# Logarithms of three chunks made in the step that sums them, and their alpha loaded one step later

## The chip, the cores and the metric

The kernel runs on one core of one Trainium2 chip. The metric is the device time of a run in microseconds. An engine is named as the profile names it: PE is TensorE (PEld its weight loads), DVE is VectorE, ACT is ScalarE, POOL is GpSimd, SP is SyncE, which here only issues DMAs.

## What is computed

The first half is a gated linear attention recurrence for 4 batches, 8 heads, 768 positions and a head width of 48. The second half is a feed-forward block on the result, 3072 tokens wide 384, with an inner width of 1024. Cut to its core, the reference is:

```python
for t in range(S):
    state = alpha[:, :, t, :, None] * state + np.einsum('bhd,bhe->bhde', k[:, :, t], v[:, :, t])
    y[:, :, t] = np.einsum('bhd,bhde->bhe', q[:, :, t], state)
x = y.transpose(0, 2, 1, 3).reshape(B * S, H * D)
a = x @ w1
b = x @ w2
h = a * b @ w3
out = h @ w_out
```

The weights arrive in float64; the rest is float32.

## The kernel before

**Chunks.** The 768 positions of a batch are cut into 6 chunks of 128, so there are 24 chunks, numbered 0 to 23 (chunk 8 is the ninth). Within a chunk the recurrence becomes matrix products: the logarithm of alpha is taken, summed over the positions with a triangular matrix, and turned back into decays that scale k and q.

**One chunk's path.** `load_a`, `load_kq` and `load_v` load alpha, k with q, and v. `logs` takes the logarithm on ACT (L302). From chunk 10 on (`LATE`), it also splits it into two parts, a copy on ACT (L306) and a difference on DVE (L307), so that the sum runs in two faster products. `decays` sums on PE (L318, L321 or L324, by the kind of chunk) and takes two exponentials on ACT (L327, L328). `decayed` scales k and q on DVE (L337). `transposed` transposes them on PE (L359) and copies them back on ACT (L361). `scores` forms the products of k and q (L399) and masks them on DVE (L402). `attend_state` applies the state (L419), `attend` the masked scores (L425), and copies the result out on ACT (L429). `outer` makes the new state (L371, then L379 or L381). `advance` decays the state on POOL (L388 to L390), from a few rows that travel through DRAM as `ends` (stores L309, L330, L332) and come back by L345.

**Pairs.** Chunks 2 to 7 come two at a time: one load of alpha and one logarithm serve two chunks, so that only even numbers load. All others load singly (L142), into the tile `ac`, which has two buffers. A load into a buffer waits until the logarithm, and the store L309 where there is one, have read what was in it.

**Steps.** The loop `for n in range(N + 1)` is the order of the work: step n computes the scores of chunk n, attends chunk n-1, transposes chunk n+1, scales chunk n+2, sums chunk n+3, and issues loads for later ones. `FIRST` is 6. Beside this, steps 0 to 6 convert w1 and w2 from float64 (L221 to L243, loads `raw` by L213); `third` makes the third part of some of these weights by two products on PE (L254, L255) and a copy on ACT (L256).

**The feed-forward part.** The results of chunks go to DRAM by `store` (`xd`), three chunks form a group, and `load_x` brings a group back (`xT`). `split_x` splits it into three parts, one on ACT (L447), two on DVE (L448, L449). `gate` multiplies it with the weights on PE (L455). From step 6 on, gates are pieces that fill PE between the recurrence's products. After the last chunk come the remaining gates, the folding of w3 with w_out, and the last projection.

**What sets the order.** Each engine and each DMA queue runs its instructions in the order in which the built program holds them. A planner derives it from the order of the calls and from its own estimate of times; `after_marks` names instructions after which a piece may stand. So a moved call may move other calls' instructions too. All matrix results go through 8 PSUM banks (`bank`), reused in turn: a product that gets a bank waits until its last reader is done. SP issues its DMAs in order, each waiting for the one that used its completion lane eight DMAs before.

The edit touches two places of the loop: the load of alpha at the step's head, and the two calls of `logs`.

Of the kernel before, what the change touches and what calls it, by code (L numbers as in the profile page):

```python
# [48 lines left out]
def kernel(  # L49
# [59 lines left out]
    def after_marks(*names):  # L109
        stack = ExitStack()  # L110
        for x in names:
            stack.enter_context(tc.issue_after(mark[x]))
        return stack
# [12 lines left out]
    def rows(src, n):  # L126
        b, c = divmod(n, NCH)
        return src[b, :, ds(c * C, C), :].rearrange("h p d -> p h d")

    def paired(n):  # L130
        return 2 <= n < PAIRED

    def load_a(n):
        if paired(n):
            if n % 2 == 0:
                b, c = divmod(n, NCH)
                x = pairs[n // 2 % 2]
                nc.sync.dma_start(out=x.rearrange("p h s d -> p h (s d)"), in_=alpha[b, :, ds(c * C, 2 * C), :].rearrange("h (p s) d -> p h (s d)", s=2))
                st["a", n] = st["a", n + 1] = x
        elif n < N:  # L140
            st["a", n] = inp.tile([C, H, D], FP32, tag="ac", name="ac", bufs=2)
            nc.sync.dma_start(out=st["a", n], in_=rows(alpha, n))  # L142

    def load_kq(n):
        if n >= N:
            return
        st["kq", n] = inp.tile([C, 2, H, D], FP32, tag="kq", name="kq")
        nc.sync.dma_start(out=st["kq", n][:, 0], in_=rows(k, n))
        nc.sync.dma_start(out=st["kq", n][:, 1], in_=rows(q, n))

    def load_v(n):
        if n < N:
            st["v", n] = vs[n % len(vs)]
            (nc.gpsimd if 2 < n < 8 else nc.sync).dma_start(out=st["v", n][:, :, 0:D], in_=rows(v, n))
# [103 lines left out]
    def fetch(ahead=3):  # L258
        while weights and len(begun) < ahead:
            begun.append(weights.popleft())  # L260
            next(begun[-1])
# [17 lines left out]
    def store():  # L279

        while later:
            dst, src = later.popleft()
            nc.sync.dma_start(out=dst, in_=src)
# [4 lines left out]
    def logs(n):  # L288
        if n >= N:
            return  # L290
        a = st.pop(("a", n))
        if paired(n):
            if n % 2 == 0:
                nc.scalar.activation(a, a, AF.Ln)
                st["la", n] = st["la", n + 1] = a
                b, c = divmod(n, NCH)
                if n in ends:
                    nc.gpsimd.dma_start(out=ends[n][2:3].rearrange("m (h d) -> m h d", h=H), in_=alpha[b:b + 1, :, c * C, :])
            return
        a = a.rearrange("p h d -> p (h d)")  # L300
        la = st["la", n] = work.tile([C, DM], FP32, tag="la", name="la")
        nc.scalar.activation(la, a, AF.Ln)  # L302
        if n >= LATE:

            t = st["la", n] = work.tile([C, 2, DM], FP32R, tag="la2", name="la2", bufs=1)
            nc.scalar.copy(t[:, 0], la)  # L306
            nc.vector.tensor_sub(t[:, 1], la, t[:, 0].bitcast(FP32))  # L307
        if n in ends:
            nc.gpsimd.dma_start(out=ends[n][2:3], in_=a[0:1])  # L309
# [83 lines left out]
    def scores(n):  # L393
        qkT = st["qkT", n]
        sc = [bank().rearrange("p (j c) -> p j c", j=NP) for _ in range(2)]
        for j in range(NP):
            for i in range(2):
                r = ds(DP * i, D)
                nc.tensor.matmul(sc[i][:, j, :], qkT[r, 0, j, :], qkT[r, 1, j, :], start=True, stop=True)  # L399
        ms = work.tile([C, 2, NP, C], FP32, tag="ms", name="ms")  # L400
        for i in range(2):
            masked = nc.vector.tensor_tensor(ms[:, i].bitcast(I32), sc[i].bitcast(I32), keep_bc, op=ALU.bitwise_and)  # L402
        ends_of_part1[0] = mark["ms", n] = masked.ins
        st["ms", n] = ms
# [3 lines left out]
    def attend_state(n):  # L408
        qkT = st.pop(("qkT", n))

        y = [bank()[:, 0:HP * C].rearrange("p (j c) -> p j c", c=C) for _ in range(2)]
        st["y", n] = y, [(half * HP + j, i, y[i][ds(DP * half, DP), j, :])
                         for j in range(HP) for i in range(2) for half in range(2)]
        if n % NCH:
            for j, i, to in st["y", n][1]:
                r = ds(DP * i, D)
                nc.tensor.matmul(to, Ts[n % 2][r, j, :], qkT[r, 1, j, :],  # L419
                                 start=(j % HP == 0), stop=False, skip_group_check=True)  # L420
# [18 lines left out]
    def load_x(g, queue=nc.sync):  # L439
        st["xT", g] = xp.tile([C, KM, TG], FP32, tag="xT", name="xT")  # L440
        queue.dma_start(out=st["xT", g], in_=xd[g].rearrange("(k p) t -> p k t", p=C))
# [157 lines left out]
    def run(pieces):  # L599

        for _ in range(pieces):
            if not fill:
                return
            try:
                next(fill[0])
            except StopIteration:
                fill.popleft()
# [22 lines left out]
    FIRST = 6  # L630
# [3 lines left out]
    for n in range(N + 1):  # L634
        store()
        if n in loads:
            load_x(loads[n])
        if n != 1:
            load_a(n + 5)
        raws = (3, 3, 3, 3, 2, 2, 3, 3)[n] if n < 8 else 4  # L640
        for m in (n + 3,) * (n <= FIRST) + (n + 4,) * (n >= FIRST):
            load_kq(m)
            if n < FIRST - 2:
                fetch(raws)
        if n >= FIRST:
            load_v(n + 2)
        if n:
            attend_state(n - 1)
        if n < N:
            scores(n)  # L650
        transposed(n + 1)
        if n == 1:
            decays(3)
            load_a(6)
            with after_marks(("e", 3)):
                logs(4)
        if n == FIRST + 1:
            run(2)
        if n < FIRST:
            with after_marks("pool"):  # L660
                load_v(n + 2)
        if n - 2 in begin and n > FIRST:
            g, tiles = begin[n - 2]
            with after_marks(("ms", n), ("qkT", n + 1)):
                split_x(g, 0)
            fill.extend(gate(g, f) for f in tiles)
        if n == FIRST:
            with after_marks("l", ("qkT", n + 1)):
                split_x(0, 0)
            fill.extend(gate(0, f) for f in begin[n - 3][1])  # L670
        pieces = ((3, 3, 2, 0) if n > FIRST + 3 else (0, 3, 3, 0))[(n - FIRST) % 4] if n >= FIRST else 0
        if n == 0:
            with after_marks(("qkT", 0)):
                logs(2)
            decays(2)
            with after_marks(("e", 2)):
                logs(3)
        early, ready = n < FIRST, len(thirds) if n > 2 else n // 2
        marks = (*[("qkT", n + 1)] * (n < N - 1), *[("qk", n + 1), ("ms", n)] * early, *["x3"] * (n - 2 in begin and n > FIRST))
        if n < N - 2 and n != FIRST:  # L680
            with after_marks(*marks):
                convert(2 if early else 1, raws)
        advance(n)
        if n:
            attend(n - 1)
        outer(n)
        if n > FIRST:
            third(ready)
        run(pieces > 0)
        if early:  # L690
            with after_marks(*marks):
                convert(1, raws)
        with after_marks(*[("ms", n)] * (n < 3)):
            decayed(n + 2)
        if not early:
            with after_marks(*[("qkT", n + 1)] * (n < N - 4)):
                logs(n + 4)
        if n == 4:
            load_x(0)
        convert(early and n > 0, raws)  # L700
        run(pieces > 1)
        if n:
            decays(n + 3)
        if n <= FIRST:
            third(ready)
        if 0 < n < FIRST:
            with after_marks(("e", n + 3)):
                logs(n + 4)
        if n == FIRST:
            with after_marks("x3", ("e", n + 3)):  # L710
                convert(2, raws)
        elif n < N - 2:
            convert(n == FIRST - 1 if early else n % 3 == 0, raws)
        if n == FIRST - 1:
            assert len(done) == 2 * KM
        run(pieces > 2)
        if n == N - 3:
            while begun:
                convert(1)
            weights.extend(load_out(j) for j in range(KF))  # L720
            fetch(4)
# [91 lines left out]
```

## Time and profile before

| | us |
|---|---|
| median of 3 runs | 473.2 |
| lowest and highest | 473.17, 474.83 |
| the profiled execution's own time | 471.82 |
| its span | 470.1 |
| PE busy | 456.8 (97%) |
| DVE busy | 358.2 (76%) |
| ACT busy | 278.6 (59%) |
| POOL busy | 78.4 (17%) |

Of the chain that ended last, 92% is PE's and 3% DMA's; L455 alone is 72% of the span. The profile's page cuts the span in 40 equal slices of some 11.75 us and gives each engine's busy share in tenths, and PE's granted clock in tenths of full speed. A timeline lists instructions in order of time: start, duration, engine, line of the kernel, operation, what it writes and reads, shapes; in brackets, how long the engine had been idle before it and what released it. A line of waits gives an engine and line, what it waited for, the total time, the number of times and the longest. A line of stretches gives for each its length, the busy time of PE, PEld, DVE, ACT and POOL with the number of instructions, then PE's granted clock, the DMA engines' share and the GB/s moved.

### The profile page before, as it was taken

Reading aid. Unit: us, or ns where it says so; the run is one execution under the profiler, and the core shown is the slowest. Engines: PE = TensorE matmul, PEld = TensorE weight load, DVE = VectorE, ACT = ScalarE, POOL = GpSimd, SP = SyncE. Lnnn points to the kernel's source line nnn. Section 1 sums busy time; section 2 is a strip of 40 time slices with the busy share of each in tenths; the row PEclk is TensorE's granted clock in tenths of the full one; section 3 lists DMA queues with packets and bytes.
Section 4 is the critical chain, followed back from the end, with each engine's and each line's share of the span. In section 5 each row is a group of like instructions: output and inputs, shape, how many; then the busy total and the mean of one; then the engine's idle time right before and its main releaser. Section 6 shows DMA issues by size and latency. Waiting matters only on the chain.

```text
span 470.1 us, 10039 instructions
## 1 busy us (share of the span) xinstructions
PE 456.8 (97%) x3848; PEld 433.3 (92%) x3848; DVE 358.2 (76%) x578; ACT 278.6 (59%) x552; POOL 78.4 (17%) x149
## 2 busy tenths in 40 slices
PE   4998999999999999999999999999999999999996
PEld 2676799999989989999999999999999999999996
DVE  2797996999969797999999968764641977766671
ACT  4686956767677464889887656644553633333330
POOL 5144212024102310222221111111111000000000
PEclk9999999999999999999999999999999999999999
DMA  9999999999999943566686432212013885555511
GB/s 179 243 216 233 237 219 207 228 225 217 218 214 222 254 124 101 178 192 203 207 287 176 158 122 101 85 50 85 33 52 117 245 238 185 175 162 167 173 52 50
DMA packets 145663, 80.29 MB, mean 171 GB/s; under 512 B 96240, under 2 KB 137456, under 8 KB 145616
## 3 DMA queue, kind: packets, MB, share of 16 engines
q1 hardware_dynamic: 139840, 64.44, 55.3%
q0 software_dynamic: 5776, 15.22, 10.4%
q8 instruction: 30, 0.49, 0.5%
q14 instruction: 17, 0.14, 0.1%
HBM read 57.58 MB, written 22.06 MB: 169 GB/s over the span
## 4 chain that ended last, share of the span: by engine, by line
PE 92%; DMA 3%; ACT 3%; DVE 1%; issue 0%; SPq 0%; DVEq 0%; ACTq 0%
PE bank L455 72%; PE bank L399 5%; PE bank L425 4%; PE bank L359 2%; PE bank L419 2%; PE bank L371 2%; PE bank L318 2%; PE bank L557 1%; DMA xd<-x 1%; PE bank L324 1%; DMA xT<-xd 1%; PE bank L321 1%; DMA ac<-in_alpha_dram 1%; DVE qk L337 0%; ACT e L327 0%
## 5 line engine op out<-in xcount | busy, mean ns | idle before, releaser
L455 PE MATMUL bank<-x,w 128*128 128x384 f32 x1152 | 211.9, 338 | 0.4 <-ACT rest L221 0.4
L455 PEld LDWEIGHTS bank<-x,w 128*128 128x128 f32 x1152 | 200.1, 188 | 2.6 <-ACT rest L221 0.7
L455 PE MATMUL bank<-w3o,ab 128*128 128x384 f32 x576 | 100.2, 336 | 0.0
L455 PEld LDWEIGHTS bank<-w3o,ab 128*128 128x128 f32 x576 | 99.9, 188 | 0.0
L480 ACT ACTIVATE bank<-bank 128x384 f32<-128x384 f32 x96 | 45.8, 477 | 41.0 <-PE bank L455 40.7
L464 ACT ACTIVATE t<-bank 128x384 f32<-128x384 f32 x64 | 31.4, 493 | 55.9 <-PE bank L455 54.7
L530 POOL DMA_DIRECT2D abd<-ab x45 | 26.1, 579 | 145.1 <-DVE ab L516 126.4
L516 DVE TENSOR_TENSOR ab<-bank,r 128x384 f32<-128x384 f32 x44 | 24.3, 553 | 25.2 <-ACT bank L480 15.2
L361 ACT COPY qkT<-bank 128x512 f32<-128x512 f32 x48 | 26.0, 591 | 23.4 <-PE bank L359 23.4
L586 DVE TENSOR_TENSOR ab<-abl,ab 128x1024 fp32r<-128x1024 f32 x24 | 29.4, 1224 | 12.8 <-ACT ab L585 12.8
L585 ACT ACTIVATE ab<-abl 128x1024 fp32r<-128x1024 f32 x24 | 25.5, 1061 | 21.0 <-PE bank L455 17.9
L455 PE MATMUL bank<-wo,w3T 128*128 128x384 f32 x192 | 35.9, 334 | 0.0
L455 PEld LDWEIGHTS bank<-wo,w3T 128*128 128x128 f32 x192 | 33.5, 188 | 0.0
L337 DVE TENSOR_TENSOR qk<-kq,e 128x768 f32<-128x768 f32 x24 | 23.5, 980 | 12.0 <-ACT e L328 8.7
L402 DVE TENSOR_TENSOR ms<-bank,keep 128x512 int32<-128x512 int32 x48 | 31.0, 680 | 0.8 <-PE bank L399 0.6
L466 DVE SCALAR_TENSOR_TENSOR o<-bank,t 128x384 f32<-128x384 f32 x24 | 13.4, 556 | 22.4 <-issue 13.8
L226 ACT ACTIVATE power<-power,rebias 128x512 uint32<-128x512 uint32 (+1 forms) x36 | 25.1, 700 | 8.9 <-DVE power L225 8.8
L587 DVE SCALAR_TENSOR_TENSOR ab<-ab,abl 128x1024 fp32r<-128x1024 f32 x24 | 29.2, 1217 | 0.0
L466 DVE SCALAR_TENSOR_TENSOR r<-bank,t 128x384 f32<-128x384 f32 x40 | 22.0, 551 | 9.5 <-ACT t L464 8.9
L399 PEld LDWEIGHTS bank<-qkT 48*128 48x128 f32 x384 | 24.3, 194 | 5.3 <-issue 2.2
L399 PE MATMUL bank<-qkT 48*128 48x128 f32 x384 | 29.0, 292 | 0.0
L425 PE MATMUL bank<-ms,v 128*64 128x128 f32 x384 | 27.1, 285 | 0.0
(88 smaller groups left out, 583.8 us busy)
## 6 DMA issues: line engine op xcount, KB each, us to landing
raw<-in_moe_w_dram SPq DMA_DIRECT2D x28, 512.0 KB, 5.4
abl<-abd SPq DMA_DIRECT2D x24, 512.0 KB, 4.4
abd<-ab POOLq DMA_DIRECT2D x45, 192.0 KB, 3.1
xT<-xd POOLq DMA_DIRECT2D x9, 576.0 KB, 4.5
kq<-in_k_dram SPq DMA_DIRECT2D x24, 192.0 KB, 5.4
kq<-in_q_dram SPq DMA_DIRECT2D x24, 192.0 KB, 5.4
xd<-x SPq DMA_DIRECT2D x48, 96.0 KB, 4.2
out_dram<-o SPq DMA_DIRECT2D x24, 192.0 KB, 3.5
```

Of the source, the lines that this page charges most:

```text
L361: mark["qkT", n] = nc.scalar.copy(qkT[:, :, :, ds(DP * half, DP)], tp[half]).ins
L399: nc.tensor.matmul(sc[i][:, j, :], qkT[r, 0, j, :], qkT[r, 1, j, :], start=True, stop=True)
L402: masked = nc.vector.tensor_tensor(ms[:, i].bitcast(I32), sc[i].bitcast(I32), keep_bc, op=ALU.bitwise_and)
L425: nc.tensor.matmul(to, vc[:, 2 * j + i, :], ms[:, i, j, :], start=(n % NCH == 0 and j % HP == 0), stop=(j % HP == HP - 1), skip_group_chec ...
L455: nc.tensor.matmul(p, w[part][i], x[part][i], start=start and part == parts[0] and i == 0, stop=stop and part == parts[-1] and i == n - 1, ...
L464: nc.scalar.activation(t, p1, AF.Copy, scale=(1.0 + 1.0 / P) * scale)
L466: nc.vector.scalar_tensor_tensor(to, p2, scale, t, op0=ALU.mult, op1=ALU.add)
L480: nc.scalar.activation(p, p, AF.Copy, scale=1.0 + 1.0 / P)
L530: (nc.gpsimd if late else nc.sync).dma_start(out=abd[g][:, f, :], in_=ab)
L585: nc.scalar.activation(t[:, 0], ab, AF.Copy, scale=1.0 - 2.0 ** -13)
L586: nc.vector.tensor_sub(t[:, 1], ab, t[:, 0].bitcast(FP32))
L587: nc.vector.scalar_tensor_tensor(t[:, 2], t[:, 0].bitcast(FP32), -1.0 - 1.0 / P, ab, op0=ALU.mult, op1=ALU.add)
```

## The change

Which alpha is loaded in which step, and in which step which logarithm is made:

| chunk | load before, after | logarithm before, after |
|---|---|---|
| 8 | step 3, 4 | end of step 4, step 5 ahead of its sum |
| 9 | step 4, 5 | end of step 5, step 6 ahead of its sum |
| 10 | step 5, 6 | step 6, step 7 ahead of its sum |
| 11 | step 6, 7 | step 7, step 7 after the sum of chunk 10 |
| 12 | step 7, 7 | step 8, 8 |

All others stay.

```diff
@@ -635,8 +635,8 @@
         store()
         if n in loads:
             load_x(loads[n])
-        if n != 1:
-            load_a(n + 5)
+        for m in {1: (), 3: (), 4: (8,), 5: (9,), 6: (10,), 7: (11, 12)}.get(n, (n + 5,)):
+            load_a(m)
         raws = (3, 3, 3, 3, 2, 2, 3, 3)[n] if n < 8 else 4
         for m in (n + 3,) * (n <= FIRST) + (n + 4,) * (n >= FIRST):
             load_kq(m)
@@ -692,9 +692,9 @@
                 convert(1, raws)
         with after_marks(*[("ms", n)] * (n < 3)):
             decayed(n + 2)
-        if not early:
+        if n > 4:
             with after_marks(*[("qkT", n + 1)] * (n < N - 4)):
-                logs(n + 4)
+                logs(n + 4 if n > FIRST + 1 else n + 3)
         if n == 4:
             load_x(0)
         convert(early and n > 0, raws)
@@ -703,7 +703,7 @@
             decays(n + 3)
         if n <= FIRST:
             third(ready)
-        if 0 < n < FIRST:
+        if 0 < n < 4 or n == FIRST + 1:
             with after_marks(("e", n + 3)):
                 logs(n + 4)
         if n == FIRST:
```

The kernel has no other difference.

## The prediction

> **What bounds the kernel now.** I read the busy slices first, then the waits and the timelines of 34 to 66 us, where the edit acts. In the page, TensorE (PE) is near full in all slices but the first and the last few:
>
> ```profile
> PE   4998999999999999999999999999999999999996
> PEclk9999999999999999999999999999999999999999
> ```
>
> By stretches, PE is busy 103.97 of the 104 us from 64 to 168 us. From 58.5 us it has no slack, so whatever it loses before shifts the end one for one. The waits of 36 to 62 us (total, times, longest) show the only large loss in the edited steps, and how VectorE (DVE) and ScalarE (ACT) wait there:
>
> ```profile
> ACT w L238 <- DVE mant L231: 3.9, 2, 3.0
> DVE qk L337 <- DMA kq<-in_q_dram: 3.3, 3, 2.4
> ...
> PE bank L419 <- POOL T L390: 2.1, 1, 2.1
> ```
>
> PE's timeline (start, length, engine, line):
>
> ```profile
> 43.79 0.67 PE L419 MATMUL bank<-qkT,T 48*64 48x128 f32 x16 [2.14 <-POOL T L390]
> ...
> 46.31 1.97 PE L425 MATMUL bank<-ms,v 128*64 128x128 f32 x16
> 48.21 1.22 PE L321 MATMUL bank<-la,sums 128*128 128x384 f32 x2
> ```
>
> L321 at 48.21 is the sums of chunk 8 (the ninth). It follows L425 at once: its logarithm was ready at 43.78. L425's 1.97 us against 1.09 elsewhere is a slow clock, seen in the stretches of 1 us (the value after the engines is the granted clock):
>
> ```profile
> 46.00:47.00 1.00, 1.00 (x14) 0.88 (x12) 0.97 (x3) 0.22 (x1) 0.00 (x0) 0.50 1.10 142
> ```
>
> The timelines of DVE, ACT and SyncE's queue (SP), in this order, give the rest:
>
> ```profile
> 38.27 1.28 DVE L402 TENSOR_TENSOR ms<-bank,keep 128x512 int32<-128x512 int32 x2
> ...
> 43.22 1.33 DVE L337 TENSOR_TENSOR qk<-kq,e 128x768 f32<-128x768 f32 x1 [2.40 <-DMA kq<-in_q_dram]
> ```
> ```profile
> 43.22 0.56 ACT L302 ACTIVATE la<-ac 128x384 f32<-128x384 f32 x1
> ...
> 49.25 0.72 ACT L226 ACTIVATE power<-power,rebias 128x512 uint32<-128x512 uint32 x1 [0.31 <-DVE power L225]
> 49.88 0.63 ACT L429 COPY x<-bank 128x256 f32<-128x256 f32 x2
> ```
> ```profile
> 34.28 0.46 SPq L142 DMA_DIRECT2D ac<-in_alpha_dram  x1
> 34.84 0.87 SPq L148 DMA_DIRECT2D kq<-in_k_dram  x1
> 35.75 1.97 SPq L149 DMA_DIRECT2D kq<-in_q_dram  x1
> ```
>
> The reader is to see that q of chunk 6 lands at 43.2, that both masks L402 of step 4 run before DVE meets that wait, and that 34.28 loads alpha of chunk 8, the load that moves.
>
> **What the Trainium skill says.** "TensorE: Matmul & The Clock Gate", Part 1 (the HAM clock gate): PE falls to half clock after an idle window of about 3.4 us and recovers after a busy one. The trace agrees: after a 2.14 us stall, half clock from 45.45 to 48.87, 3.4 us. The same page, on the array's architecture, says that DVE and ACT queues are strict FIFO; the trace agrees, ACT's L238 holding all behind it for 3.0 us. "DMA: Bandwidth & Descriptors", "Issuing engines are not separate DMA queues": loads of all queues share 16 engines. Here the DMA share is 1.03 to 1.29 in every microsecond from 40 to 51, so a load less speeds those behind it.
>
> **The change part by part.** No work is added or removed. Alpha of chunks 8, 9, 10 loads one step later (step 7 issues 11 and 12), and their logarithms go from the step before to the step of their sums. In the built order PE's sequence is unchanged. What moves:
>
> *DVE.* L337 of chunk 6 now stands ahead of step 4's two L402, L240, L222, L225; L337 of chunk 7 ahead of step 5's L402. DVE then waits for q with the masks behind it; behind those are L225, ACT's L226, and a PE product L254 that waits for a mask's bank.
>
> *ACT.* The logarithm of chunk 8 (L302) leaves step 4 and stands in step 5 behind L429, L226, L429; that of chunk 9 leaves step 5 and stands in step 6 behind L447 and both L429. PE's L321 stands right after L425 and now waits for them: a new wait.
>
> *SP.* One load fewer is ahead of kq of chunk 6: 0.197 MB at the window's 224 GB/s is 0.9 us, so q lands at 42.3; by issue, right behind k at about 34.8, plus the 6.3 us median of q's landing, 41.1. I take 41.7. For chunk 7 I take 47.7, between 47.3 and 48.2 (before: just in time for L337 at 49.15).
>
> First wait, from start-to-start times of the same DVE timeline: 41.7 + L337 0.88 + two L402 1.20 + L240 0.60 + L222 0.34 gives L225 at 44.7. L381 0.29, L228 0.60, L229 0.73, L231 0.7 bring DVE to 47.4. L337 of chunk 7 at 47.7, + 0.88 + 1.20 + 0.60 + 0.34 is L225 at 50.7, ended at 51.15. ACT: L226 at 51.2 (+0.63), L429 (+0.27), L302 at 52.1, ended at 52.65. PE's L321 starts at 52.7 where it was 48.21: **+4.5 us**.
>
> Clock: PE is idle from 47.2 or so to 52.7, so it restarts at half speed. A whole window costs half of 3.4: **+1.7**.
>
> Second wait: warm, PE from L321 to L359 takes 0.46 + 0.47 + 0.60 + 1.09 + 0.50 = 3.12, cold 4.8, to 57.5. ACT copies qkT (0.94), L447 (1.07), two L429 (0.54), L302 (0.56), hand-overs 0.15: 60.75 for L321 of chunk 9, 7.26 later than the 53.49 of before. PE's own work in between is 4.59 warm, 6.3 cold, so the second wait is 60.75 - 52.7 - 6.3 = **+1.75**; the 0.69 that the slow clock cost in this stretch before (5.28 - 4.59) comes off.
>
> Given back: from L321 of chunk 9 to L425 of step 7, before took 60.77 - 53.49 = 7.28, with waits for q of chunk 8 and for the split x. The work is 0.46 + 0.94 + 1.09 + 0.50 + 3.34 = 6.33. The split now ends at about 62.3 and PE asks for it only from 63.7: **-0.95**.
>
> Sum: 4.5 + 1.7 + 1.75 - 0.69 - 0.95 = **+6.3 us**.
>
> At nothing: on ACT and DVE, L306 (0.40) and L307 (0.55) of chunk 10 move into step 7, under 3.3 us of L455; without that cover they add 0.95. On GpSimd (POOL), L309 waits for the later alpha and holds L332 and the load of v of chunk 7 by some 2 us; v lands near 53.5, wanted at 61.7 or later. On SP, the load of alpha 10 in step 5 had waited for a buffer until 48.56 (idle since 46.75); alpha 9 need not, which brings kq of chunk 8 forward, but PE is already late. In step 7 alpha 12 waits for chunk 10's logarithm and holds kq of 11, v of 9 and stores; they are wanted a step or two (some 9 us each) later.
>
> Profiled: 471.8 + 6.3 = 478.1 (span 470.1, 1.7 around it). The median shown, 473.2, is 1.4 above that; I forecast 473.2 + 6.3 = **479.5**.
>
> **Bounds.** q of chunk 6 at 40.2 and of chunk 7 by 46.2 take 1.5 off; landings of 42.3 and 48.2 add 0.5. The clock loss is 0 to 1.7 at the first wait, and 0 to 1.7 at the second, whose 1.75 idle of a 3.4 window is as much as the share that set it off before. The likeliest's own range is 477.5 to 480.5.
>
> **The rivals.** *Both waits cool the clock:* 479.5 + 1.7 = 481.2. For it: the idle share just named; against: a busy stretch straddles the window. *DVE's order does no harm:* if q of chunk 6 lands before 39, L321 waits only for two L429 and L302 after L425, 1.3, then 1.75, less 0.95 and the clock's 0.69: +1.4, so 474.6. Against: nothing in the view lands 4 us sooner for one load less. *Faster:* the freed DMA time lets the values of `ends` land early, the 2.14 stall falls under the point where the clock drops, and 2.14 + 1.7 = 3.8 is won: 469.4. This decides if POOL's L390 ends by about 42 and the logarithm of chunk 8 is ready when L425 ends (48.3); but that logarithm stands behind the copy of that L425. *The change does less than it says:* no; the built order shows the moves.
>
> **How the numbers follow.** Main case 0.60, both cold 0.22, no harm 0.09, faster 0.04, a longer landing or other wait 0.05. 0.5% is 2.4 us, about what a measurement can tell from no change. Slower 0.88, within it 0.08, faster 0.04. The range, 475.8 to 482.0, leaves out the last two cases and part of the first's early-landing end.
>
> **What would show it.** Right: PE idle of over 3 us ahead of L321 near 52 us, released by ACT's L302; a second of 1 to 2 us near 60; L337 ahead of L402 on DVE near 41; half clock after 52; PE then full. Wrong: L321 following L425 at once, or L425 of step 7 before 63.

## The result, and the profile after

The changed kernel takes **480.24 us** (median of 6 runs, 477.82 to 481.36) where the kernel before takes 473.2 (6 runs, 472.72 to 474.83): a ratio of **1.0137 [1.0118, 1.0156]**, slower by 7.0 us. The forecast was 479.5. The profiled execution took 481.36, with a span of 479.6: 9.5 us above the profiled execution of before. A second profile of the same kernel has a span of 477.4 (own time 479.08), 7.3 above. Both differences count some 1.4 us too much, as the profiled execution of before, with 471.82, was a quick one, and the first profile is that of the slowest of the six runs. The two profiles differ in a way that matters, so I show both.

The busy slices of the changed kernel:

```profile
PE   4997699999999999999999999999999999999996
PEclk9999579999999999999999999999999999999999
```

The fourth and fifth slices (36 to 60 us) have lost work, and the clock now has a dent in the fifth and sixth. From there on PE is as full as before: a stretch shows it busy 99.96 of the 100 us from 68 to 168 us. The whole loss lies in some 25 us, around the edited steps.

The waits of 36 to 70 us (engine, line, what it waited for; total, times, longest):

```profile
PE bank L321 <- ACT la L302: 6.2, 2, 5.7
...
ACT power L226 <- DVE power L225: 5.3, 2, 3.6
...
DVE qk L337 <- ACT x L429: 2.9, 1, 2.9
```

The first line is new: the sums of chunks 8 and 9 wait for the logarithm on ACT. The second names what stood ahead of that logarithm. PE's wait for POOL's L390, 2.1 before, is gone; in its place PE's L254 waits 1.55 for a mask. PE's timeline of the changed kernel:

```profile
42.67 0.50 PE L254 MATMUL bank<-w,signs 128*128 128x512 f32 x1 [1.55 <-DVE ms L402]
...
45.51 1.09 PE L425 MATMUL bank<-ms,v 128*64 128x128 f32 x16
...
52.27 1.65 PE L321 MATMUL bank<-la,sums 128*128 128x384 f32 x2 [5.67 <-ACT la L302]
...
58.63 1.97 PE L425 MATMUL bank<-ms,v 128*64 128x128 f32 x16
...
61.92 1.65 PE L321 MATMUL bank<-la,sums 128*128 128x384 f32 x2 [0.49 <-ACT la L302]
...
70.30 1.09 PE L425 MATMUL bank<-ms,v 128*64 128x128 f32 x16
```

L321 of chunk 8 starts at 52.27 after 5.67 idle us. L425 still lasts 1.97 us at 58.63 and L321 still 1.65 at 61.92: PE stayed at half clock for 13 us after it had work again. DVE's and ACT's timelines of the changed kernel, in this order, show the chain behind the 5.67:

```profile
41.06 0.96 DVE L337 TENSOR_TENSOR qk<-kq,e 128x768 f32<-128x768 f32 x1 [2.87 <-ACT x L429]
41.94 1.28 DVE L402 TENSOR_TENSOR ms<-bank,keep 128x512 int32<-128x512 int32 x2
...
47.35 0.96 DVE L337 TENSOR_TENSOR qk<-kq,e 128x768 f32<-128x768 f32 x1 [0.65 <-DMA kq<-in_q_dram]
48.23 1.28 DVE L402 TENSOR_TENSOR ms<-bank,keep 128x512 int32<-128x512 int32 x2
...
50.36 0.42 DVE L225 TENSOR_SCALAR power<-raw 128x512 uint32<-128x512 uint32 x1
```
```profile
50.81 0.72 ACT L226 ACTIVATE power<-power,rebias 128x512 uint32<-128x512 uint32 x1 [1.66 <-DVE power L225]
51.44 0.35 ACT L429 COPY x<-bank 128x256 f32<-128x256 f32 x1
51.69 0.52 ACT L302 ACTIVATE la<-ac 128x384 f32<-128x384 f32 x1
...
58.77 1.07 ACT L361 COPY qkT<-bank 128x512 f32<-128x512 f32 x2 [3.38 <-PE bank L359]
59.73 1.18 ACT L447 ACTIVATE x<-xT 128x1152 fp32r<-128x1152 f32 x1
60.80 0.65 ACT L429 COPY x<-bank 128x256 f32<-128x256 f32 x2
61.31 0.56 ACT L302 ACTIVATE la<-ac 128x384 f32<-128x384 f32 x1
```

Read it upwards from the logarithm of chunk 8, L302 at 51.69: it stands behind a copy L429, that behind L226, L226 waits for DVE's L225, and L225 stands behind L337, which began when q of chunk 7 had landed. The last four lines are the second wait: the logarithm of chunk 9 stands behind copies of which the first, L361, waits 3.38 us for PE's own product L359. The first L337 is put down to an ACT copy that had just ended and that it doesn't read. The traces point to the load instead: q of chunk 6, issued at 34.21, took 6.3 us to land (40.5), and L337 began half a microsecond later, the same distance as in the run with the loads alone, where the profile names the load (issued at 35.96, 7.8 us to landing, L337 at 44.29).

PE's timeline of the second profile of the change:

```profile
52.62 1.65 PE L321 MATMUL bank<-la,sums 128*128 128x384 f32 x2 [5.73 <-ACT la L302]
...
57.84 1.09 PE L425 MATMUL bank<-ms,v 128*64 128x128 f32 x16
...
61.15 0.91 PE L321 MATMUL bank<-la,sums 128*128 128x384 f32 x2 [1.76 <-ACT la L302]
...
67.86 1.09 PE L425 MATMUL bank<-ms,v 128*64 128x128 f32 x16
```

The first wait is the same. The clock is back by 57.84 (L425 1.09), and the second wait is 1.76 instead of 0.49. L425 of step 7, the last line, stands 2.4 us earlier than in the first profile, and the span is 2.2 us shorter. Cut at three points, the loss against before is:

| | predicted | first profile | second profile |
|---|---|---|---|
| L321 of chunk 8, before 48.21 | +4.5 | +4.06 | +4.41 |
| from it to L321 of chunk 9, before 5.28 | +2.76 | +4.37 | +3.25 |
| from it to L425 of step 7, before 7.28 | -0.95 | +1.10 | -0.57 |
| sum | +6.31 | +9.53 | +7.09 |
| span, before 470.1 | | +9.5 | +7.3 |

The sum meets the difference of the spans within 0.2 us. It does so, within 0.3, in each experiment below that keeps a late logarithm: what L425 of step 7 has lost is what the kernel has lost.

### The profile page after: what moved, and what is told of

It is laid out like the page before. It is cut to its first block, busy times and chain, and to the rows that moved or that the text cites. A ratio compares the mean times of both kernels' runs of the same rounds, so it can differ in the third digit from the quotient of the medians.

```text
span 479.6 us, 10041 instructions
## 1 busy us (share of the span) xinstructions
PE 461.0 (96%) x3848; PEld 436.2 (91%) x3848; DVE 359.0 (75%) x578; ACT 279.6 (58%) x552; POOL 78.0 (16%) x149
## 4 chain that ended last, share of the span: by engine, by line
PE 91%; DVE 3%; ACT 2%; DMA 2%; issue 1%; SPq 1%; DVEq 0%; ACTq 0%
PE bank L455 70%; PE bank L399 5%; PE bank L425 4%; PE bank L359 2%; PE bank L419 2%; PE bank L371 2%; PE bank L557 1%; DMA kq<-in_q_dram 1%; PE bank L321 1%; PE bank L324 1%; PE bank L318 1%; DVE qk L337 1%; DVE ms L402 1%; DMA ac<-in_alpha_dram 1%; DVE w L240 0%
## 5 line engine op out<-in xcount | busy, mean ns | idle before, releaser
L455 PE MATMUL bank<-x,w 128*128 128x384 f32 x1152 | 211.7, 338 | 0.1
L455 PEld LDWEIGHTS bank<-x,w 128*128 128x128 f32 x1152 | 200.2, 188 | 1.9 <-issue 0.5
L455 PE MATMUL bank<-w3o,ab 128*128 128x384 f32 x576 | 100.2, 336 | 0.0
L455 PEld LDWEIGHTS bank<-w3o,ab 128*128 128x128 f32 x576 | 99.9, 188 | 0.0
L361 ACT COPY qkT<-bank 128x512 f32<-128x512 f32 x48 | 25.9, 592 | 26.9 <-PE bank L359 26.9
L455 PE MATMUL bank<-wo,w3T 128*128 128x384 f32 x192 | 35.9, 334 | 0.0
L402 DVE TENSOR_TENSOR ms<-bank,keep 128x512 int32<-128x512 int32 x48 | 31.1, 681 | 3.5 <-PE bank L399 3.4
L455 PEld LDWEIGHTS bank<-wo,w3T 128*128 128x128 f32 x192 | 33.5, 188 | 0.0
L226 ACT ACTIVATE power<-power,rebias 128x512 uint32<-128x512 uint32 (+1 forms) x36 | 25.1, 699 | 13.3 <-DVE power L225 13.1
L337 DVE TENSOR_TENSOR qk<-kq,e 128x768 f32<-128x768 f32 x24 | 22.9, 953 | 12.6 <-ACT e L328 8.9
L425 PE MATMUL bank<-ms,v 128*64 128x128 f32 x384 | 27.1, 285 | 0.0
```

What stands on the lines that cost most here:

```text
L337: mark["qk", n] = nc.vector.tensor_mul(qks[n % 3][:, :, :, 0:D], st.pop(("kq", n)), st.pop(("e", n)).rearrange("p i (h d) -> p i h d", h=H ...
L361: mark["qkT", n] = nc.scalar.copy(qkT[:, :, :, ds(DP * half, DP)], tp[half]).ins
L425: nc.tensor.matmul(to, vc[:, 2 * j + i, :], ms[:, i, j, :], start=(n % NCH == 0 and j % HP == 0), stop=(j % HP == HP - 1), skip_group_chec ...
L455: nc.tensor.matmul(p, w[part][i], x[part][i], start=start and part == parts[0] and i == 0, stop=stop and part == parts[-1] and i == n - 1, ...
```

## The experiments

Each kernel ran in several rounds beside the kernel before on the same chip; the ratio given is to that. Two theories stood against each other. **The place of the logarithms:** they stand on ACT behind conversions and copies that themselves wait for DVE and PE, so PE's sums wait. **The order on DVE and the loads:** the later alpha moves L337 ahead of the masks, and that delay is the loss. A third question is what the half clock costs.

### The logarithms' places alone

The loads of before, with the rest of the change:

```diff
-        for m in {1: (), 3: (), 4: (8,), 5: (9,), 6: (10,), 7: (11, 12)}.get(n, (n + 5,)):
-            load_a(m)
+        if n != 1:
+            load_a(n + 5)
```

> The logarithms of chunks 8 to 10 are moved as in the change, the loads of alpha stay as before. In the built order DVE keeps the order of before in steps 4 and 5 (masks L402 ahead of L337); on ACT the logarithm of chunk 8 stands behind both L429 of step 5. Theory A (the place of the logarithms on ACT makes the new wait of PE): L321 of chunk 8 starts at 49.5 to 50.5 us instead of 48.21, the one of chunk 9 at 56 to 58.5 instead of 53.49; +2.5 us with a warm clock, up to +6 if PE cools: 475.5 to 479. Theory B (DVE's order, the wait for q ahead of the masks, makes it): the order is that of before, so 473 to 474.

Measured: 478.48 (5 runs), ratio 1.0098 [1.0076, 1.0120]. Its PE timeline:

```profile
50.66 1.65 PE L321 MATMUL bank<-la,sums 128*128 128x384 f32 x2 [4.37 <-ACT la L302]
...
60.32 0.91 PE L321 MATMUL bank<-la,sums 128*128 128x384 f32 x2 [0.94 <-ACT la L302]
```

DVE's order is that of before (first mask L402 at 38.55, L337 of chunk 6 at 43.27), and the loss is there: some 5 of the 7 us, with both waits. The two sums came later than I had expected (50.5 and 58.5 at the latest), the second by nearly 2 us, as half clock lasted 10.24 us in this execution.

### The loads alone

The new line of loads in the kernel before, whose logarithms stay where they were:

```diff
-        if n != 1:
-            load_a(n + 5)
+        for m in {1: (), 3: (), 4: (8,), 5: (9,), 6: (10,), 7: (11, 12)}.get(n, (n + 5,)):
+            load_a(m)
```

> The loads of alpha are one step later as in the change, the logarithms stay in the step before their sums. In the built order DVE has the order of the change in steps 4 and 5 (L337 ahead of the masks), ACT makes the logarithm of chunk 8 at the end of step 4. Theory A: L321 of chunk 8 follows L425 within 1 us, near 47 to 49; the end within +-1 us of before, 472.5 to 474.5. Theory B: PE waits as in the change, L321 near 52, 478 to 481.

Measured: 473.27 (14 runs), ratio 0.9999 [0.9983, 1.0014]. The profiled execution is the slowest of them (475.76); q of chunk 6 landed late in it. Its PE timeline shows the DVE order at work:

```profile
45.90 0.80 PE L254 MATMUL bank<-w,signs 128*128 128x512 f32 x1 [4.57 <-DVE ms L402]
...
52.66 0.91 PE L321 MATMUL bank<-la,sums 128*128 128x384 f32 x2
```

PE waits for the mask that stands behind L337, and L321 then follows at once, as its logarithm ran at 49.62. That moment is later than the 47 to 49 that I had expected, and in this execution the order on DVE does cost: L425 of step 7 stands at 64.31, 3.5 us later than in the profile of before. The median is that of before: over 14 runs the moved loads and the order on DVE cost nothing by themselves.

### The logarithms ahead of the copies

The change, with the logarithms of chunks 8 and 9 in the same steps 5 and 6, but at their heads:

```diff
+        if n in (5, 6):
+            logs(n + 3)
...
-        if n > 4:
+        if n > FIRST:
```

> The change, but the logarithms of chunks 8 and 9 are called at the head of steps 5 and 6, ahead of the products of the step; the built order has that of chunk 8 on ACT right after L226 of step 4, before L327, and DVE's order is that of the change. Theory A: the logarithm is ready before L425 ends, no wait for it, L321 of chunk 8 near 47 to 48.5; 473 to 475. Theory B: L225 and the copies are as late as in the change, so PE still waits for later things, 477 to 480.

Measured: 473.02 (14 runs), ratio 0.9998 [0.9981, 1.0014]. In the profile L321 of chunk 8 starts at 51.82 and that of chunk 9 at 56.97, neither with a wait for ACT. The time is what the place of the logarithms predicts. The moment is not: I had expected L321 by 48.5; in this execution (474.66) PE waited 4.03 us for a mask, as with the loads alone. So, with DVE in the order of the change, neither the later load of alpha nor the step in which the logarithm is called costs the 7 us: what stands ahead of it in ACT's queue does. A call at the head of a step is early in that queue: the logarithm of chunk 8 runs at 47.56, ahead of step 4's L327, and that of chunk 9 right after L256, where it stood in the kernel before. The logarithms of chunks 10 and 11 stand here as in the change, so their move costs nothing.

### Chunk 8's logarithm alone at the head

As before, but for chunk 8 only; chunk 9's stays behind L447 and both L429:

```diff
+        if n == 5:
+            logs(n + 3)
...
-        if n > 4:
+        if n > 5:
```

> The change with the logarithm of chunk 8 alone called at the head of its step; that of chunk 9 stays where the change has it, behind L447 and both L429. By my sum the wait of chunk 8 is most of the loss and that of chunk 9 1.75 us less the 0.95 given back: 473.5 to 475. Rival (each wait costs by itself, with its own slow clock): 475.5 to 478.

Measured: 475.59 (22 runs), ratio 1.0053 [1.0036, 1.0070]. PE's timeline:

```profile
49.01 0.91 PE L321 MATMUL bank<-la,sums 128*128 128x384 f32 x2
...
57.31 0.91 PE L321 MATMUL bank<-la,sums 128*128 128x384 f32 x2 [2.66 <-ACT la L302]
...
65.51 1.09 PE L425 MATMUL bank<-ms,v 128*64 128x128 f32 x16
```

The second wait alone costs 2.5 us, which is more than my sum had left for it (475 at most) and lies in the range of the rival, that each wait costs by itself. It is 2.66 here and not 1.76, as PE comes to it earlier, and it is followed by a window of half clock (58.62 to 62.03). If the two waits add up, the first one carries the rest, 4.5 of 7 us; no run has the first wait alone.

### DVE in the order of before

The change, with L337 held behind the masks, as before:

```diff
-        with after_marks(*[("ms", n)] * (n < 3)):
+        with after_marks(*[("ms", n)] * (n < 6)):
             decayed(n + 2)
```

> The change, with L337 of steps 3 to 5 held behind the masks of its step, so that DVE has the order of before and no mask waits for q; loads and logarithms are the change's. Theory A with the DVE chain as its length (my sum): L321 of chunk 8 starts at 48.8 to 50, of chunk 9 at 55 to 57.5; +1.5 with a warm clock to +5: 474.5 to 478. Theory B' (the late logarithm alone makes the whole loss): as the change, 479 to 481.

Measured: 477.21 (7 runs), ratio 1.0076 [1.0045, 1.0108]. PE's timeline:

```profile
49.24 1.65 PE L321 MATMUL bank<-la,sums 128*128 128x384 f32 x2 [3.38 <-ACT la L302]
...
57.53 0.91 PE L321 MATMUL bank<-la,sums 128*128 128x384 f32 x2 [1.75 <-ACT la L302]
```

Both waits for the logarithm stay, but the first one ends 3 us earlier, since L225 no longer stands behind an L337 that waits for q. So the order on DVE is worth some 3 us of the 7, within some 2 us either way, **but only through the late logarithm**: with the logarithm early (the loads alone) it is worth nothing in the median. In this execution half clock lasts one window, 49.10 to 52.51, but it is one of the quick ones (475.52). The seven line up by their mean granted clock: 474.62 and 475.52 us at 0.995, 476.91 to 477.88 at 0.989, and 480.66 at 0.977.

### The clock: products that fill PE's wait

To take the half clock away and leave the wait, constant products (`ident` by `sums`, 128x256, float32, into the bank that L321 then overwrites) are put ahead of the sums of chunks 8 and 9: 14 and 5, in later kernels 8 and 4, then 9 and 0. They are extra work. The inserted line moves the lines below it by one, so that the sums, L321 elsewhere, are L322 here.

```diff
+            for x in [0] * {8: 14, 9: 5}.get(n, 0): nc.tensor.matmul(lc[:, 0:2 * C], ident, sums[:].rearrange("p s t -> p (s t)").bitcast(FP32), start=True, stop=True)
```

> The change, with 14 products of two constants (some 0.3 us each) ahead of L321 of chunk 8 and 5 ahead of that of chunk 9, into the bank that L321 then overwrites: PE works through most of both waits instead of standing idle, all else in steps 4 to 6 stands as in the change. Theory C (of the change's loss, 6.4 us of the profiled 9.5 is half clock, set off by the idle PE): the clock stays full, L321 of chunk 8 near 52, L425 of step 7 near 65 instead of 70.3; 474.5 to 476.5. Rival (the engines behind PE set the time, the clock hides in their waits): within 1 us of the change, 479 to 481.

> As the longer filler, with 8 and 4 products: a product took 0.44 us in that run, so 14 (6.2 us) had outlasted the wait. 8 are 3.5 us, 4 are 1.8, inside the waits of 5.7 and 1.75. Theory C (half clock is in the time): clock full or one window at most, L321 of chunk 8 at 51 to 52.5, L425 of step 7 near 65; 474.8 to 477. Rival: as the change, 479 to 481.

> Only the first wait filled, with 9 products (4.0 us); nothing else of the built order of steps 4 to 6 moves. Theory C: PE stays warm over the first wait, the second wait of 1.75 us stands and may bring one window; L425 of step 7 at 65 to 67; 475 to 478. Rival: as the change, 479 to 481.

Measured: 480.35 (5 runs), ratio 1.0132 [1.0099, 1.0165]; 478.86 (6 runs), 1.0125 [1.0098, 1.0153]; 479.5 (6 runs), 1.0145 [1.0111, 1.0178]. The first and the last lie in the rival's range, the second just below it, and none in theory C's. PE's timeline with 14 and 5:

```profile
48.59 6.31 PE L321 MATMUL bank<-sums,ident 128*128 128x256 f32 x28
54.74 0.81 PE L322 MATMUL bank<-la,sums 128*128 128x384 f32 x2
```

The products outlast the wait: the logarithm was there by 51.4, the sums start at 54.74. The clock was full from 47.92 on, but the overrun cost what the clock gave. With 8 and 4 the sums start at 52.36, after a last idle of 2.04 us, and the half clock moves to 53.63 to 60.46. With 9 and 0, q came late and the half clock sits at 45.70 to 52.52 and 62.76 to 66.18. None is the clean test that I wanted: **how much of the 7 us is the clock is not settled by these.** They bound it, though. One execution of each had a mean granted clock of 0.999 or 1: 478.04, 476.36 and 477.25 us, still 5.0, 3.5 and 4.4 above the median of before. So a large part of the loss is there without half clock (the first of them with the overrun in it). The slowest executions of each, at 0.988 to 0.992, took 3 to 5 us more than these. That is again a correlation, as what makes PE idle also makes the clock fall.

### The cover in the kernel before

The kernel before has a cold window too. Does it cost anything there, or does it lie under a later wait that would have held PE anyway (the cover)? Six such products ahead of L419 of step 5 (lines below move by one), with L337 held:

```diff
+        for x in [0] * (6 if n == 4 else 0): nc.tensor.matmul(y[0].rearrange("p j c -> p (j c)"), ident, sums[:].rearrange("p s t -> p (s t)").bitcast(FP32), start=True, stop=True)
...
-        with after_marks(*[("ms", n)] * (n < 3)):
+        with after_marks(*[("ms", n)] * (n < 7)):
```

> The kernel before, with 6 products of two constants (some 0.3 us each) ahead of L419 of step 5, where PE waits 2.14 us for L390; L337 of steps 3 to 6 is held behind the masks so that DVE's order stays that of before. Theory C: no half clock from 45 to 49, 1.7 us less: 471.5 to 472.3. Rival (DVE and ACT set this stretch, PE's slow clock lies under them): 473 to 474.

Measured: 472.83 (22 runs), ratio 0.9992 [0.9978, 1.0006]. A stretch and PE's timeline:

```profile
40.00:60.00 20.00, 18.66 (x217) 14.71 (x217) 16.52 (x28) 15.50 (x35) 5.77 (x10) 1.00 1.01 233
```
```profile
58.81 2.32 PE L456 MATMUL bank<-x,w 128*128 128x384 f32 x12 [0.56 <-DVE x L450]
```

The clock (the third value from the end) is 1.00 throughout, and nothing is gained that can be told from noise (I had expected 1.7 us): PE waits for L450, which is the last part of the split of x (L449 elsewhere). In the kernel before, the same wait (0.36 at 58.53) is put down to ACT's L221, which the gate doesn't read, but DVE's L449 ends at 58.38 there. So the split, and not PE, sets when PE is full; DVE in turn runs without a gap from L337 of chunk 8, which waits for q until 54.62, to the end of the split.

### The early stall taken away

Is the 2.14 us stall on POOL's L390 worth anything? In the kernel before, the load of v in step 4 goes behind `advance`:

```diff
-        if n < FIRST:
+        if n < FIRST and n != 4:
...
+        if n == 4:
+            with after_marks("pool"):
+                load_v(n + 2)
```

> The kernel before, with POOL's load of v in step 4 (0.9 us of issue) put behind L390 instead of ahead of it; nothing else moves. The state is ready 0.9 to 1.2 us earlier, PE's stall at L419 shrinks from 2.14 to about 1, and the half clock may not come: 470.5 to 472.5. Rival (the next wait takes its place: q of chunk 6 and the masks' banks): 473 to 474.

Measured: 472.38 (22 runs), ratio 0.9983 [0.9969, 0.9997]. The stall fell to 1.44 us, half clock still came (43.65 to 47.06), and PE still waits before a gate at 58.58. This is the only version whose interval lies below the kernel before, by 0.17% and barely. Its profile doesn't show where the gain comes from: L425 of step 7 stands at 60.84, where before it stood at 60.77.

### All of it together

The logarithms at the heads of their steps, the loads of the change, L337 held (`n < 7`) and v behind `advance`:

> The loads of the change, with what the runs showed to be harmless or of use: the logarithms of chunks 8 and 9 at the head of their step, L337 of steps 3 to 6 held behind the masks, POOL's load of v in step 4 behind L390. Theory A and the freed load together: q of chunk 6 lands near 41 to 42, the state is ready by 42, no wait for a logarithm; 471 to 472.5, below both kernels. Rival (the split of x on ACT and DVE sets the moment when PE is full, and it is no earlier): 472.5 to 473.5.

Measured: 473.09 (14 runs), ratio 0.9999 [0.9983, 1.0015]. PE's timeline:

```profile
42.37 0.67 PE L419 MATMUL bank<-qkT,T 48*64 48x128 f32 x16 [0.62 <-POOL T L390]
...
47.21 0.91 PE L321 MATMUL bank<-la,sums 128*128 128x384 f32 x2 [1.51 <-ACT e L328]
...
54.26 0.91 PE L321 MATMUL bank<-la,sums 128*128 128x384 f32 x2 [0.96 <-ACT la L302]
...
59.86 2.33 PE L455 MATMUL bank<-x,w 128*128 128x384 f32 x12 [0.57 <-DVE x L449]
```

ACT's timeline:

```profile
45.88 0.52 ACT L302 ACTIVATE la<-ac 128x384 f32<-128x384 f32 x1 [2.64 <-DMA ac<-in_alpha_dram]
...
53.68 0.52 ACT L302 ACTIVATE la<-ac 128x384 f32<-128x384 f32 x1 [1.38 <-DMA ac<-in_alpha_dram]
```

PE reaches L321 of chunk 8 a microsecond earlier than before, but that of chunk 9 at 54.26, where before it stood at 53.49: I had expected no wait for a logarithm, and both logarithms now wait for their alpha, 2.64 and 1.38 us. So the later load of alpha does have a price once neither DVE nor ACT hides it, and the early gain is gone before the split of x. This version therefore doesn't test what the split would have left of that gain. Nothing tried beats the kernel before by more than 0.17%.

### The change once more

> The change itself once more, for a second profile beside the shorter fillers on one chip: 478 to 482 with PE idle ahead of both L321, half clock after the first wait for one to five windows of 3.4 us. If the half clock is shorter than in the first profile, the span should be shorter by half of the difference.

Measured: 479.58 (4 runs), ratio 1.0154 [1.0129, 1.0179]; its trace is the second profile above. The mean granted clock of an execution tells how long half clock lasted: 0.982 of 479 us is 17 us, 0.992 some 8. The six executions at 0.981 or 0.982, over both comparisons, took 480.3 in the mean, the two at 0.991 and 0.992 took 478.5. So a long half clock goes with some 2 us more. Between the two profiles half clock differs by 10.24 us, and I had expected the span to differ by half of that, 5.1; it differs by 2.2. Part of the slow time fell on PE's idle waits, where it costs nothing, and the second wait was 1.27 us shorter where PE came later. The remaining two, at 0.985 and 0.988, took 481.3 and 479.5. That is a correlation over ten executions, not a cause shown.

## Why the prediction was right, and where its steps were not

- **The first wait, +4.5.** Right in place, size and cause: 52.27 and 52.62 for a predicted 52.7, released by ACT's L302. Its links came as said: L225 at 44.07 and 50.36 (predicted 44.7, 50.7), L302 at 51.69 (52.1), q of chunk 7 at 47.35 (47.7). That the place of the logarithm is the cause is shown: the logarithms' places alone lose 5 us, and put ahead of the conversions and copies they lose none.
- **DVE's order.** The rival that it does no harm is refuted in its size: some 3 us go when it is undone.
- **The second wait, +1.75.** 1.76 at 61.15 (predicted 60.75) in the second profile; 0.49 at 61.92 in the first, where PE was still slow and so came later. Alone it costs 2.5.
- **PE's own work, 0.38 too small in two places.** The prediction counts L254 with L255 as 0.47 and two such pairs as 0.94. The timeline of before, from start to start, has 0.85 and 1.32:

```profile
48.97 0.69 PE L254 MATMUL bank<-w,signs 128*128 128x512 f32 x1
49.50 0.40 PE L255 MATMUL bank<-w,signs 128*128 128x512 f32 x1
49.82 0.67 PE L419 MATMUL bank<-qkT,T 48*64 48x128 f32 x16
...
53.94 0.69 PE L254 MATMUL bank<-w,signs 128*128 128x512 f32 x1
...
55.26 1.16 PE L399 MATMUL bank<-qkT 48*128 48x128 f32 x16
```

- **The 0.69 that came off.** It should have been 0.31. PE's work from L321 of chunk 8 to that of chunk 9 is 4.97 at full clock, not 4.59, and before had only 0.65 us of half clock left after 48.21.
- **Given back, -0.95.** -0.57 in the second profile: the split no longer holds PE, as said, and the difference is the 0.38 (6.71 of work, not 6.33). In the first it was +1.10, as the same work took 8.38, a part of it at half clock.
- **The clock, +1.7: mis-sized too.** I let half clock end after one window. I also read the half clock of before as agreeing with what I had cited, an idle window of some 3.4 us; only its length agrees, as PE had stood idle for 2.14 us there and not for a whole window. In the second profile it ended at 56.45, and the work between the two sums took 6.77 where it is 4.97 at full clock: 1.8 lost, as forecast, although half clock had begun earlier and lasted two windows. In the first it lasted to 65.61 and took 4.2 from that work and 1.7 from the stretch behind it, 5.9 in all; 1.3 came back from the second wait. The rival "both waits cool the clock" had the sign and about the time of some executions, but not the way: in both profiles the first cold period went on or ended, and no second one began.
- **The sum, in part luck.** With 0.31 and 0.57 in place of 0.69 and 0.95 it is +7.1, which is the second profile's +7.09. The recorded +6.3 came near the measured 7.0 although these two terms were 0.76 short and the clock term ranged from 1.8 to 5.9.
- **Work hidden.** L306 and L307 of chunk 10 ran at 69.57 and 70.58, beside L455 and L425, with no wait. POOL's L309 waited 1.82 (predicted some 2), and the load of v of chunk 7 was issued at 47.13; PE never waited for it. On SP, alpha 12 did wait in step 7, as said, and nothing on PE followed.
- **Not foreseen:** PE's wait for POOL's L390 went, and one of 1.55 for a mask's bank took its place. I had named L254 behind the mask and priced nothing for it. Neither shows at the end, as PE waits for the logarithm until 52.27 anyway.
- **"Faster", by way of that stall.** Its 3.8 us were not won by any version: taking 0.7 of the stall away gave 0.7 us, just outside the noise; making the clock full gave nothing that can be measured; and both with the logarithms ahead gave nothing, there because alpha came too late. With the clock full, PE waited for the split.

## What to carry to other kernels

An instruction is as late as the queue that it is put in: a short ACT instruction that PE needs next should stand ahead of, not behind, work that waits for another engine (here a conversion that waits for DVE) or for PE's own last product, since otherwise each engine waits for the other in turn. Calling for a value "in the step that uses it" cost nothing here at the head of the step, where it stands ahead of that work and its input has landed, and 7 us behind it. Before pricing an early stall as a gain, look for the later meeting point that sets the moment: in this kernel the split of x covers some early stalls of PE, and the delays measured at L425 of step 7, behind the split, were those of the whole kernel.

## What the runs showed of the hardware that was not expected

The granted clock stayed low while PE had work. Stretches of 1 us of the changed kernel's first profile:

```profile
52.00:53.00 1.00, 0.73 (x1) 0.50 (x2) 0.95 (x2) 0.21 (x1) 0.00 (x0) 0.50 1.15 280
...
55.00:56.00 1.00, 1.00 (x18) 0.67 (x13) 0.82 (x1) 0.39 (x1) 0.24 (x1) 0.50 1.15 231
...
60.00:61.00 1.00, 1.00 (x18) 1.00 (x16) 0.00 (x0) 1.00 (x2) 0.08 (x1) 0.50 1.32 148
...
64.00:65.00 1.00, 1.00 (x3) 0.45 (x2) 1.00 (x4) 1.00 (x3) 0.00 (x0) 0.50 1.00 246
```

PE (the first busy value) is 1.00 in each microsecond from 53 to 61, and again at 64, and the clock is 0.50 in all of them. Half clock ran from 48.55 to 65.61, which is 17.07 us or five windows of 3.41. In the second profile it was two windows (6.83), with the logarithms' places alone three (10.24), in the kernel before and in the profile with DVE held one. "TensorE: Matmul & The Clock Gate", Part 1 (the HAM clock gate), in the Trainium skill, has PE recover after a busy window of that length; here several windows that the profile calls busy did not bring the clock back, and the measurement decides. Why, the runs don't show. Beside it, the landing of q of chunk 6 varied: L337 waited for it until 44.29 with the loads alone and had no wait at 41.03 with DVE held. The load was issued at 35.96 and 34.27 and took 7.8 and 6.4 us to land, behind the same loads in the same order.
